# A windowed-attention and gated feed-forward kernel: first loads on two hardware queues, the second half masked by products

## The chip, the cores and the metric

One of the eight cores of a Trainium2 chip runs the whole program. The metric is device time in microseconds (us): the kernel before takes 258.63 us, the median of three runs (257.68 to 258.73).

## The reference

Attention over four batches, eight heads, 768 positions and 64 values per head, then a feed-forward layer. A query sees the last 96 positions up to its own and the first eight positions of all ("global"); a slope per head times the distance is taken from the scores.

```python
scores = scale * np.matmul(q, k.transpose(0, 1, 3, 2))
dist = np.where(is_global & ~is_local, float(n_local), np.abs(rel))
scores = np.where(is_global | is_local, scores - slopes * dist, -1e9)
a = softmax(scores); x = a @ v          # (B, H, S, D), then laid out as 3072 x 512
out = (np.maximum(x @ w_gate, 0) * (x @ w_val)) @ w_out
```

The weights are 512 x 1536 twice and 1536 x 512; the output is 3072 x 512 in float32.

## The kernel before, in words

The 3072 tokens are eight chunks of 384 (two halves `s` of each batch). A chunk goes through scores, exponential, weighted sum of values, normalisation (logarithm, exponential of its negative, product: lines 450 to 455) into `xT`, and then through the feed-forward pieces `gate`, `val` and `outp` (L477, L487, L496). A gate is four matmuls over the four 128-row parts of `xT`, one per pair of heads, so its fourth matmul needs the last pair of the chunk. `gate` is followed by a ReLU on ScalarE (L480), `val` by a product on VectorE (L489).

The order of all instructions is written out by hand; each engine works its own list in order. From chunk 2 on, a function `weave` lays attention pieces between feed-forward pieces. Chunks 0 and 1 are different, since nothing is there yet to lie beside them. All of the change is in these two.

**Chunk 0** (the code from L540 to L595). Its keys and queries come in three pairs of loads on the SyncE queue (`load_first`, L181: heads 0-1, 2-3, 4-7, keys before queries), its values with one load on GpSimd's queue (L216). GpSimd builds an index table `rel`, the distances `dd` (L198 to L202), the identity `ident` (L206), the table `sidx`, and then issues the load of the values. VectorE patches eight rows of `dd`, makes `diag` tiles (identity times a slope, L232) and casts the loaded rows to bfloat16 (L284); TensorE turns them (L275, "transposes"); copies bring them into `kT` and `qT` (L262 to L264, L292). `first_scores` (L311) puts two things into one PSUM tile `s_ps`: `diag` times `dd`, which adds slope times distance and the mask (L321), and then keys times queries (L330). ScalarE takes the exponential into `ef` (L336). `first_values` (L307) picks the value rows with products by `sel`. `first_av` (L440) sums the values (once with ones, for the denominator); `first_norm` follows. `keep_busy` (L538) are matmuls on zeros.

In the written order the transposes of heads 4-5 (`first_keys(2)`) stand ahead of the scores of heads 2-3. GpSimd casts heads 6-7 and issues the first two weight loads (L153) and the loads of chunk 1 (L562).

**Chunk 1** (L605 to L619). The pieces of its attention stand between the first twelve feed-forward pieces of chunk 0 (`F[0]` to `F[11]`: gate and val of six of the twelve column groups). `second_keys` (K) is 12 transposes, two copies on VectorE (L300, L301) and three on GpSimd (L266 to L268). SC is `first_scores` for one of two groups of a head pair. PSUM has two `ff` tiles, one `s_ps` tile and four `t` tiles in this stretch, so that the next scores wait for the exponential of the last. After it, the steady part begins with the gate of group 6 of chunk 0.

Chunks from 2 on use no `diag`: they multiply the exponential by a table `m_all` on VectorE (L393). That table is made by eight exponentials on ScalarE (`make_mask`, L242), woven between the feed-forward pieces that follow chunk 1 (L635).

Of the kernel before, what the change touches and what calls it, by code (L numbers as in the profile page):

```python
# [15 lines left out]
def kernel(  # L16
# [87 lines left out]
    def w_of(t, dc, fc):  # L104
        f = fc % GW
        return t[fc // GW][:, dc, f * 128 : (f + 1) * 128]
# [68 lines left out]
    def rows_of(src, s, h0, h1):  # L175
        b, half = divmod(s, 2)
        return src[b, h0:h1, half * QH : (half + 1) * QH, :].rearrange("h (p n) d -> p h (n d)", n=NN)

    def load_first(h0, h1):
        for i, src in enumerate((k, q)):  # L180
            nc.sync.dma_start(out=kq0[:, i, h0:h1, :], in_=rows_of(src, 0, h0, h1))  # L181

    load_first(0, 2)
    load_first(2, 4)
# [1 line left out]
    nc.scalar.preload_act_table_set("natural_log_exp_and_others")  # L186

    zeros = firstp.tile([128, 512], BF16)
    nc.vector.memset(zeros.bitcast(mybir.dt.uint32), 0)
    nc.vector.memset(ident, 0.0)  # L190
    nc.vector.memset(ones, 1.0)


# [1 line left out]
    rel = firstp.tile([128, NN, WQ], FP32)  # L195
    sub = firstp.tile([128, NN, WQ], FP32)
    near = [firstp.tile([NG, NN, WQ], FP32, name=f"near{i}") for i in range(2)]
    nc.gpsimd.iota(rel, [[1, NN], [NN, WQ]], base=NG, channel_multiplier=-1,  # L198
                   allow_small_or_imprecise_dtypes=True)
    nc.gpsimd.affine_select(out=sub, in_=rel, compare_op=ALU.is_ge, fill=BIG, base=NG,  # L200
# [5 lines left out]
    nc.gpsimd.affine_select(out=ident, in_=ident, compare_op=ALU.not_equal,  # L206
                            fill=1.0, base=0, pattern=[[-1, 128]],
                            channel_multiplier=1)
# [25 lines left out]
    def clear_keys(p):  # L234
        nc.vector.memset(kT[0][p][:, 3, 32:128].bitcast(mybir.dt.uint32), 0)
        nc.vector.memset(kT[0][p][:, 6, NG + 48 : 128].bitcast(mybir.dt.uint32), 0)

    def make_sel(n):
        nc.vector.tensor_scalar(sel[:, n], sidx, float(n), None, op0=ALU.is_equal)
# [71 lines left out]
    def first_scores(s, p, g):  # L311
        half = s % 2
        spans_ = [by[half, j] for j in steps_of[half][g]]
        ps = psum["s"].tile([128, 2, 512], FP32, name="s_ps")
        es = ef_pool.tile([128, 2, 360], BF16, name=f"ef{g}")
        cols = sum(NN * w for _, _, w, _ in spans_)
        qd = qTb[s][:, p, 0, :].rearrange("d (n t) -> d n t", n=NN)
        for e in range(2):
            c = 0
            for i, (j, a, w, m) in enumerate(spans_):  # L320
                nc.tensor.matmul(ps[:, e, c : c + NN * w].rearrange("k (n t) -> k n t", n=NN),  # L321
                                 lhsT=diag[:, 2 * p + e],
                                 rhs=dd[:, 0 if j == 0 else 1, :, m : m + w],
                                 start=(i == 0), stop=False, skip_group_check=True)
                c += NN * w
        c = 0
        for i, (j, a, w, m) in enumerate(spans_):
            for e in range(2):
                r = slice(64 * e, 64 * e + 64)
                nc.tensor.matmul(ps[:, e, c : c + NN * w].rearrange("k (n t) -> k n t", n=NN),  # L330
                                 lhsT=kT[0][p][r, j, :], rhs=qd[r, :, a : a + w],
                                 start=False, stop=(i == len(spans_) - 1),
                                 skip_group_check=True)
            es_of[s, p, j] = (es, c)
            c += NN * w
        nc.scalar.activation(es[:, :, 0:cols], ps[:, :, 0:cols], AF.Exp, bias=0.0, scale=scale)  # L336

    def piece_cast_k(s, p):
        nc.gpsimd.tensor_copy(  # L339
# [126 lines left out]

    out_v = out.rearrange("(s p n) d -> s n p d", p=128, n=NN)

    def ffn_pieces(c):
        ht = ht_pool.tile([128, N_FC, QH], BF16, name="ht")  # L470
        st = {}

        def gate(fc):
            xT = xT_of[c]
            psg = psum["ff"].tile([128, 512], FP32, name="ff_ps")
            for dc in range(N_DC):
                nc.tensor.matmul(psg[:, 0:QH], lhsT=w_of(wg, dc, fc), rhs=xT[:, dc, :],  # L477
                                 start=(dc == 0), stop=(dc == N_DC - 1))
            gr = gr_pool.tile([128, QH], BF16, name="grelu")
            nc.scalar.activation(gr, psg[:, 0:QH], AF.Relu, bias=0.0, scale=1.0)  # L480
            st["gr"] = gr

        def val(fc):
            xT = xT_of[c]
            psv = psum["ff"].tile([128, 512], FP32, name="ff_ps")
            for dc in range(N_DC):
                nc.tensor.matmul(psv[:, 0:QH], lhsT=w_of(wv, dc, fc), rhs=xT[:, dc, :],  # L487
                                 start=(dc == 0), stop=(dc == N_DC - 1))
            nc.vector.tensor_tensor(ht[:, fc, :], psv[:, 0:QH], st["gr"], op=ALU.mult)  # L489

        def outp(n, part):
            if part == 0:
                st["o"] = psum["ff"].tile([128, 512], FP32, name="ff_ps")
            ps2 = st["o"]
            for fc in range(part * N_FC // 2, (part + 1) * N_FC // 2):
                nc.tensor.matmul(ps2, lhsT=ht[:, fc, n * 128 : (n + 1) * 128],  # L496
                                 rhs=wo_sb[:, fc, :],
                                 start=(fc == 0), stop=(fc == N_FC - 1))
            if part == 1:
                osb = osb_pool.tile([128, DM], FP32, name="osb")  # L500
# [52 lines left out]
    clear_keys(1)  # L553
    keep_busy(3)
    first_keys(1, A)
    keep_busy(2)
    first_cast(3, 0, P)
    load_w_group(0)
    first_cast(3, 1, P)
    for h0 in (0, 4):  # L560
        for i, src in enumerate((k, q)):
            nc.gpsimd.dma_start(out=kq1[:, i, h0 : h0 + 4, :], in_=rows_of(src, 1, h0, h0 + 4))  # L562
    for j in (4, 5, 6, 3):
        load_v(0, j)
    first_scores(0, 0, 0)
    make_sel(1)
    first_cast(2, 0, V)
    first_cast(2, 1, V)
    clear_keys(2)
    first_scores(0, 0, 1)  # L570
    first_keys(2, V)
    make_sel(2)
# [32 lines left out]
    stack = open_psum(ff=2, s=1, t=4)  # L605
    f1_0, f2_0 = ffn_pieces(0)
    f1_1, f2_1 = ffn_pieces(1)
    F = [f for _, f in f1_0]
    K = [lambda p=p: second_keys(p) for p in range(HP)]

    def SC(p, g):
        return lambda: first_scores(1, p, g)
# [77 lines left out]
```

## Time and profile before

| What | Time |
|---|---|
| median of three runs | 258.63 us |
| the profiled execution | 259.5 us, its span 257.7 us |
| TensorE busy | 245.1 us (95% of the span) |
| ScalarE, VectorE, GpSimd busy | 155.0, 130.0, 91.9 us |
| the gate of the last pair's `xT` for chunk 0 (L477 at its fourth matmul) | starts at 24.06 us |
| the gate of group 6, where the steady part begins | starts at 45.08 us |
| last matmul's copy (L501) | starts at 253.94 us |

All times in the views are microseconds from the start of the span. Busy times are sums over an engine's instructions. A row of the timeline gives start, length, engine, line, operation, output and input, and in brackets the idle time before it with what ended it. A row of a table by windows gives for each engine the busy time and the number of instructions in that stretch; PEclk is the granted TensorE clock, 1.00 being full. A row of the chain of waits gives start and length of a piece of the chain that ended last.

### The profile page before, as it was taken

The numbers are of one execution on the slowest core, as the hardware profiler recorded it, in microseconds if no ns is written. First come the engines' busy times: TensorE is split into PE (matmuls) and PEld (weight loads), VectorE is DVE, ScalarE is ACT, GpSimd is POOL, SyncE is SP. The second block draws the span as 40 slices with busy tenths as digits, with TensorE's granted clock in tenths as the row PEclk, the third lists the DMA queues.
The fourth block names the chain that finished last, engine by engine and source line by source line (L and its number), as shares of the span: only waits on it lengthen the run. The fifth ranks groups of instructions, "written<-read, shape, count | busy, mean of one in ns | idle before, by whom it ended". The sixth has DMA issues, their size and how long they took to land.

```text
span 257.7 us, 4900 instructions
## 1 busy us (share of the span) xinstructions
PE 245.1 (95%) x1757; PEld 143.3 (56%) x1766; DVE 130.0 (50%) x330; ACT 155.0 (60%) x308; POOL 91.9 (36%) x227
## 2 busy tenths in 40 slices
PE   7797988999999999999999999999999999999993
PEld 3355654665554566655665566556665566556641
DVE  6764405374643377625674376624763457614410
ACT  2536466833577577756875577747774677643311
POOL 6674494066844606800744236500640000000000
PEclk9889999999999999999999999999999999999999
DMA  6999999958966993775693987926491200021012
GB/s 177 158 197 178 206 138 150 256 143 152 268 109 172 185 299 78 135 81 179 175 112 53 201 248 123 107 84 211 116 145 41 81 3 0 1 84 41 0 43 81
DMA packets 80232, 33.59 MB, mean 130 GB/s; under 512 B 58192, under 2 KB 77136, under 8 KB 80208
## 3 DMA queue, kind: packets, MB, share of 16 engines
q1 hardware_dynamic: 48464, 24.57, 37.7%
q0 software_dynamic: 31744, 8.71, 32.9%
q8 instruction: 14, 0.23, 0.4%
q14 instruction: 10, 0.08, 0.1%
HBM read 28.41 MB, written 6.29 MB: 135 GB/s over the span
## 4 chain that ended last, share of the span: by engine, by line
PE 83%; ACT 6%; DVE 5%; DMA 3%; issue 1%; SPq 1%; ACTq 0%; DVEq 0%
PE ff_ps L496 24%; PE ff_ps L487 22%; PE ff_ps L477 22%; PE av_ps L409 5%; PE qk_ps L381 4%; DMA kq<-in_q_dram 3%; DVE xT L426 2%; PE s_ps L321 2%; ACT ef L336 2%; DVE ht L489 2%; PE t_ps L307 1%; PE s_ps L330 1%; PE t_ps L275 1%; ACT lnd L418 1%; SPq L181 1%
## 5 line engine op out<-in xcount | busy, mean ns | idle before, releaser
L477 PE MATMUL ff_ps<-xT,wg 128*128 128x384 bf16 x384 | 78.4, 326 | 1.6 <-DVE xT L455 0.9
L487 PE MATMUL ff_ps<-xT,wv 128*128 128x384 bf16 x384 | 78.1, 326 | 1.0 <-DVE ht L489 0.8
L480 ACT ACTIVATE grelu<-ff_ps 128x384 bf16<-128x384 f32 x96 | 46.9, 489 | 36.0 <-DVE ht L489 18.6
L489 DVE TENSOR_TENSOR ht<-ff_ps,grelu 128x384 bf16<-128x384 f32 x96 | 53.2, 555 | 28.2 <-PE ff_ps L487 22.8
L496 PE MATMUL ff_ps<-wo_sb,ht 128*128 128x512 bf16 x279 | 66.3, 379 | 0.5
L426 DVE TENSOR_TENSOR xT<-av_ps,rcp 64x384 bf16<-64x384 f32 x48 | 26.6, 555 | 46.1 <-ACT rcp L423 41.6
L477 PEld LDWEIGHTS <-wg 128*128 128x128 bf16 x384 | 36.1, 97 | 24.7 <-issue 1.7
L487 PEld LDWEIGHTS <-wv 128*128 128x128 bf16 x384 | 36.1, 97 | 24.7 <-issue 3.2
L393 DVE TENSOR_TENSOR es<-es,m_all 128x432 bf16<-128x432 bf16 (+5 forms) x108 | 33.5, 339 | 22.9 <-ACT es L384 22.4
L384 ACT ACTIVATE es<-qk_ps 128x432 bf16<-128x432 f32 (+2 forms) x72 | 37.8, 528 | 10.7 <-PE qk_ps L381 8.9
L496 PEld LDWEIGHTS <-ht 128*128 128x128 bf16 x288 | 26.9, 97 | 27.8
L339 POOL CAST kc<-ks 128x384 bf16<-128x384 f32 x24 | 12.0, 541 | 59.1 <-DMA ks<-in_k_dram 47.2
L418 ACT ACTIVATE lnd<-av_ps 64x384 f32<-64x384 f32 x48 | 23.3, 485 | 11.0 <-PE av_ps L409 10.4
L501 ACT COPY osb<-ff_ps 128x512 f32<-128x512 f32 x24 | 14.0, 585 | 24.4 <-PE ff_ps L496 23.5
L381 PE MATMUL qk_ps<-qT,kT 128*128 128x432 bf16 (+5 forms) x108 | 24.7, 286 | 0.0
L409 PEld LDWEIGHTS <-vbuf 128*128 128x128 bf16 x216 | 18.1, 98 | 8.2 <-issue 0.7
L136 POOL DMA_DIRECT2D vbuf<-in_v_dram x25 | 21.6, 875 | 1.7 <-DMA wv<-in_moe_w_val_dram 1.1
L409 PE MATMUL av_ps<-es,vbuf 128*128 128x216 bf16 (+4 forms) x216 | 21.1, 226 | 0.5 <-DVE xT L426 0.5
L336 ACT ACTIVATE ef<-s_ps 128x720 bf16<-128x720 f32 (+2 forms) x16 | 11.2, 708 | 11.6 <-PE s_ps L330 11.4
L347 POOL CAST qz<-qs 128x192 bf16<-128x192 f32 x48 | 14.8, 357 | 4.3 <-DMA qs<-in_q_dram 4.3
L381 PEld LDWEIGHTS <-kT 128*128 128x128 bf16 x108 | 10.6, 98 | 7.8
L423 ACT ACTIVATE rcp<-lnd 128x384 f32<-128x384 f32 x24 | 12.5, 523 | 0.8
(80 smaller groups left out, 142.7 us busy)
## 6 DMA issues: line engine op xcount, KB each, us to landing
out_dram<-osb SPq DMA_DIRECT2D x24, 256.0 KB
ks<-in_k_dram SPq DMA_DIRECT2D x6, 768.0 KB
qs<-in_q_dram SPq DMA_DIRECT2D x6, 768.0 KB
vbuf<-in_v_dram POOLq DMA_DIRECT2D x21, 120.0 KB, 4.7
wg<-in_moe_w_gate_dram POOLq DMA_DIRECT2D x3, 512.0 KB, 8.0
wv<-in_moe_w_val_dram POOLq DMA_DIRECT2D x3, 512.0 KB, 10.2
wo_sb<-in_moe_w_out_dram POOLq DMA_DIRECT2D x1, 1536.0 KB, 15.1
kq<-in_k_dram SPq DMA_DIRECT2D x2, 192.0 KB
```

The costliest lines, as they stand in the source:

```text
L136: nc.gpsimd.dma_start(out=v_dst(b, NG + r0, NG + r0 + n, j), in_=v[b, :, KT * j + r0 : KT * j + r0 + n, :].rearrange("h p d -> p h d"))
L381: nc.tensor.matmul(ps[:, c : c + n_], lhsT=kt[:, j, :], rhs=qd[:, :, :, a : a + w], start=True, stop=True)
L384: nc.scalar.activation(es[:, 0:cols], ps[:, 0:cols], AF.Exp, bias=0.0, scale=scale)
L393: nc.vector.tensor_mul(e4, e4, mk)
L409: nc.tensor.matmul(av3[:, :, a : a + w], lhsT=vb[:, j, z0 : z0 + 128], rhs=es[:, c : c + NN * w].rearrange("k (n p) -> k n p", n=NN), star ...
L418: nc.scalar.activation(ln[o0 : o0 + 64], av[d0 : d0 + 64, 0:QH], AF.Ln, bias=0.0, scale=1.0)
L426: nc.vector.tensor_tensor(xT_of[s][r, p, :], av_of[s, p, e_][r, 0:QH], rc[r], op=ALU.mult)
L477: nc.tensor.matmul(psg[:, 0:QH], lhsT=w_of(wg, dc, fc), rhs=xT[:, dc, :], start=(dc == 0), stop=(dc == N_DC - 1))
L480: nc.scalar.activation(gr, psg[:, 0:QH], AF.Relu, bias=0.0, scale=1.0)
L487: nc.tensor.matmul(psv[:, 0:QH], lhsT=w_of(wv, dc, fc), rhs=xT[:, dc, :], start=(dc == 0), stop=(dc == N_DC - 1))
L489: nc.vector.tensor_tensor(ht[:, fc, :], psv[:, 0:QH], st["gr"], op=ALU.mult)
L496: nc.tensor.matmul(ps2, lhsT=ht[:, fc, n * 128 : (n + 1) * 128], rhs=wo_sb[:, fc, :], start=(fc == 0), stop=(fc == N_FC - 1))
```

## The change

There are four edits, and nothing changes from the gate of group 6 on except that the eight `make_mask` exponentials are gone from there.

- **First loads.** Keys go on SyncE's queue and queries on ScalarE's. The load of the values moves to the head of GpSimd's list, and `ident` to the place after it. The clears of `kT` move from VectorE to GpSimd. The first weight loads (`load_w_group(0)`) and half of chunk 1's loads move ahead of GpSimd's casts. The cast of heads 2-3's queries moves from ScalarE to VectorE.
- **Order in chunk 0.** The scores of heads 2-3 now stand ahead of the transposes of heads 4-5. Two of the eight `make_mask` move to ScalarE's start.
- **Masks by products.** For chunk 1, `first_scores` leaves out its `diag` matmuls; `first_masks` multiplies the exponentials by `m_all` on VectorE. The other six `make_mask` stand between the pieces of chunk 1.
- **Split first gate, and an order of chunk 1.** The first three matmuls of `gate(0)` and `val(0)` run as `begin`, the fourth of each after it. The first sums of chunk 1 (`AV[0]`) stand between the last scores.

The program's lists agree: TensorE has 40 matmuls and their weight loads less, VectorE 20 products more. ScalarE has three load issues more and one cast less, SyncE three loads less.

```diff
     def load_first(h0, h1):
-        for i, src in enumerate((k, q)):
-            nc.sync.dma_start(out=kq0[:, i, h0:h1, :], in_=rows_of(src, 0, h0, h1))
+        for i, (src, eng) in enumerate(((k, nc.sync), (q, nc.scalar))):
+            eng.dma_start(out=kq0[:, i, h0:h1, :], in_=rows_of(src, 0, h0, h1))
...
+    nc.gpsimd.dma_start(out=v3, in_=rows_of(v, 0, 0, H))
+    nc.gpsimd.affine_select(out=ident, in_=ident, ...)
     nc.gpsimd.iota(rel, [[1, NN], [NN, WQ]], base=NG, ...)
...
-    nc.gpsimd.affine_select(out=ident, in_=ident, ...)
...
-    nc.gpsimd.memset(vbuf[0][:, NT - 1, :].bitcast(mybir.dt.uint32), 0)
-    nc.gpsimd.dma_start(out=v3, in_=rows_of(v, 0, 0, H))
+    for p in range(HP):
+        nc.gpsimd.memset(kT[0][p][:, 3, 32:128].bitcast(mybir.dt.uint32), 0)
+        nc.gpsimd.memset(kT[0][p][:, 6, NG + 48 : 128].bitcast(mybir.dt.uint32), 0)
...
-        for e in range(2):
+        for e in range(2) if half == 0 else ():
             c = 0
             for i, (j, a, w, m) in enumerate(spans_):
                 nc.tensor.matmul(ps[...], lhsT=diag[:, 2 * p + e], ...)
...
+    def first_masks(s, p, g):
+        for j in steps_of[s % 2][g]:
+            _, a, w, m = by[s % 2, j]
+            es, c = es_of[s, p, j]
+            for_all = es[:, :, c : c + NN * w]
+            mk = m_all[:, 2 * p : 2 * p + 2, 0 if j == 0 else 1, :, m : m + w]
...
+            nc.vector.tensor_mul(for_all, for_all, mk)
...
+        def begin():
+            product(wg, "g", 0, 0, N_DC - 1)
+            product(wv, "v", 0, 0, N_DC - 1)
+        begin_of[c] = (begin, lambda: gate(0, N_DC - 1), lambda: val(0, N_DC - 1))
...
     keep_busy(9)
+    load_w_group(0)
     make_diag(0)
     make_diag(1)
-    clear_keys(0)
+    make_mask(0)
+    make_mask(1)
     first_cast(0, 0, V)
     first_cast(0, 1, V)
     make_sel(0)
     first_cast(1, 0, V)
-    first_cast(1, 1, A)
+    first_cast(1, 1, V)
     first_keys(0, A)
...
     first_keys(1, A)
     keep_busy(2)
-    first_cast(3, 0, P)
-    load_w_group(0)
-    first_cast(3, 1, P)
+    first_scores(0, 0, 0)
+    make_sel(1)
+    first_scores(0, 0, 1)
+    make_sel(2)
+    first_cast(2, 0, V)
+    first_cast(2, 1, V)
     for h0 in (0, 4):
         for i, src in enumerate((k, q)):
             nc.gpsimd.dma_start(out=kq1[:, i, h0 : h0 + 4, :], ...)
+        if h0 == 0:
+            first_cast(3, 0, P)
+            first_cast(3, 1, P)
...
     first_scores(0, 1, 0)
     for h in range(4, H):
         make_diag(h)
-    clear_keys(3)
     first_scores(0, 1, 1)
+    first_keys(2, V)
     first_values(0, V)
     first_keys(3, V)
...
-    F = [f for _, f in f1_0]
+    F = list(begin_of[0]) + [f for _, f in f1_0[2:]]
+    M = [lambda h=h: make_mask(h) for h in range(H)]
...
-    for f in (F[0], F[1], K[0], F[2], K[1], SC(0, 0), F[3], SC(0, 1), K[2], F[4], SC(1, 0), K[3], F[5],
-              SC(1, 1), SC(2, 0), F[6], SC(2, 1), AV[0], SC(3, 0), N[0], AV[1], SC(3, 1), N[1], F[7],
-              lambda: load_qk_after(2), AV[2], F[8], N[2], AV[3], F[9], N[3], F[10], F[11]):
+    for f in (F[0], F[1], F[2], M[2], M[3], K[0], F[3], K[1], SC(0, 0), F[4], SC(0, 1), M[4], K[2], SC(1, 0), F[5],
+              M[5], SC(1, 1), K[3], F[6], M[6], SC(2, 0), AV[0], N[0], M[7], SC(2, 1), F[7], AV[1], N[1],
+              SC(3, 0), F[8], SC(3, 1), AV[2], N[2], lambda: load_qk_after(2), F[9], AV[3], N[3],
+              F[10], F[11], F[12]):
         f()
...
-    weave(f1_1[G[0]], spread([(0.0, lambda h=h: make_mask(h)) for h in range(H)], 0.0, 1.0))
+    weave(f1_1[G[0]])
```

In the new list SC(p, g) is the scores followed by `first_masks`, F[0] is `begin`, F[1] and F[2] are the fourth matmuls of the first gate and val with their ReLU and product.

More of the change, by code (lines that the diff above doesn't have):

```diff
@@ L188 @@
     zeros = firstp.tile([128, 512], BF16)
+    nc.vector.memset(ident, 0.0)
     nc.vector.memset(zeros.bitcast(mybir.dt.uint32), 0)
-    nc.vector.memset(ident, 0.0)
     nc.vector.memset(ones, 1.0)
@@ L197 @@
     near = [firstp.tile([NG, NN, WQ], FP32, name=f"near{i}") for i in range(2)]
+    nc.gpsimd.dma_start(out=v3, in_=rows_of(v, 0, 0, H))
+    nc.gpsimd.affine_select(out=ident, in_=ident, compare_op=ALU.not_equal,
+                            fill=1.0, base=0, pattern=[[-1, 128]],
+                            channel_multiplier=1)
     nc.gpsimd.iota(rel, [[1, NN], [NN, WQ]], base=NG, channel_multiplier=-1,
@@ L205 @@
                             channel_multiplier=1)
-    nc.gpsimd.affine_select(out=ident, in_=ident, compare_op=ALU.not_equal,
-                            fill=1.0, base=0, pattern=[[-1, 128]],
-                            channel_multiplier=1)
     sidx = firstp.tile([128, 4, 128], FP32, name="sidx")
@@ L232, in make_diag @@
         nc.vector.tensor_scalar(diag[:, h], ident, -slopes[h] / scale, None, op0=ALU.mult)
-    def clear_keys(p):
-        nc.vector.memset(kT[0][p][:, 3, 32:128].bitcast(mybir.dt.uint32), 0)
-        nc.vector.memset(kT[0][p][:, 6, NG + 48 : 128].bitcast(mybir.dt.uint32), 0)
     def make_sel(n):
@@ L331, in first_scores @@
                                  lhsT=kT[0][p][r, j, :], rhs=qd[r, :, a : a + w],
-                                 start=False, stop=(i == len(spans_) - 1),
+                                 start=(i == 0 and half == 1), stop=(i == len(spans_) - 1),
                                  skip_group_check=True)
@@ L336, in first_scores @@
         nc.scalar.activation(es[:, :, 0:cols], ps[:, :, 0:cols], AF.Exp, bias=0.0, scale=scale)
+    def first_masks(s, p, g):
[4 more added lines that the diff above has]
+            mk = m_all[:, 2 * p : 2 * p + 2, 0 if j == 0 else 1, :, m : m + w]
+            if w == WQ:
+                mk = mk.rearrange("k e n p -> k e (n p)")
+            else:
+                for_all = for_all.rearrange("k e (n p) -> k e n p", n=NN)
+            nc.vector.tensor_mul(for_all, for_all, mk)
     def piece_cast_k(s, p):
@@ L467 @@
     out_v = out.rearrange("(s p n) d -> s n p d", p=128, n=NN)
+    begin_of = {}
     def ffn_pieces(c):
@@ L471, in ffn_pieces, with product, gate @@
         st = {}
[L473 to L477, printed above, removed]
+        def product(w, key, fc, d0, d1):
+            if d0 == 0:
+                st[key] = psum["ff"].tile([128, 512], FP32, name="ff_ps")
+            for dc in range(d0, d1):
+                nc.tensor.matmul(st[key][:, 0:QH], lhsT=w_of(w, dc, fc), rhs=xT_of[c][:, dc, :],
                                  start=(dc == 0), stop=(dc == N_DC - 1))
+        def gate(fc, d0=0):
+            product(wg, "g", fc, d0, N_DC)
+            psg = st["g"]
             gr = gr_pool.tile([128, QH], BF16, name="grelu")
@@ L481, in gate, with val @@
             st["gr"] = gr
[L483 to L488, printed above, removed]
+        def val(fc, d0=0):
+            product(wv, "v", fc, d0, N_DC)
+            psv = st["v"]
             nc.vector.tensor_tensor(ht[:, fc, :], psv[:, 0:QH], st["gr"], op=ALU.mult)
@@ L552 @@
     make_diag(3)
-    clear_keys(1)
     keep_busy(3)
@@ L562 @@
             nc.gpsimd.dma_start(out=kq1[:, i, h0 : h0 + 4, :], in_=rows_of(src, 1, h0, h0 + 4))
+        if h0 == 0:
+            first_cast(3, 0, P)
+            first_cast(3, 1, P)
+    nc.gpsimd.memset(vbuf[0][:, NT - 1, :].bitcast(mybir.dt.uint32), 0)
     for j in (4, 5, 6, 3):
         load_v(0, j)
[L565 to L572, printed above, removed]
     first_scores(0, 1, 0)
@@ L607, with run @@
     f1_1, f2_1 = ffn_pieces(1)
-    F = [f for _, f in f1_0]
+    F = list(begin_of[0]) + [f for _, f in f1_0[2:]]
     K = [lambda p=p: second_keys(p) for p in range(HP)]
+    M = [lambda h=h: make_mask(h) for h in range(H)]
     def SC(p, g):
-        return lambda: first_scores(1, p, g)
+        def run():
+            first_scores(1, p, g)
+            first_masks(1, p, g)
+        return run
     AV = [lambda p=p: first_av(1, p) for p in range(HP)]
     N = [lambda p=p: first_norm(1, p) for p in range(HP)]
-    for f in (F[0], F[1], K[0], F[2], K[1], SC(0, 0), F[3], SC(0, 1), K[2], F[4], SC(1, 0), K[3], F[5],
-              SC(1, 1), SC(2, 0), F[6], SC(2, 1), AV[0], SC(3, 0), N[0], AV[1], SC(3, 1), N[1], F[7],
-              lambda: load_qk_after(2), AV[2], F[8], N[2], AV[3], F[9], N[3], F[10], F[11]):
+    for f in (F[0], F[1], F[2], M[2], M[3], K[0], F[3], K[1], SC(0, 0), F[4], SC(0, 1), M[4], K[2], SC(1, 0), F[5],
+              M[5], SC(1, 1), K[3], F[6], M[6], SC(2, 0), AV[0], N[0], M[7], SC(2, 1), F[7], AV[1], N[1],
+              SC(3, 0), F[8], SC(3, 1), AV[2], N[2], lambda: load_qk_after(2), F[9], AV[3], N[3],
+              F[10], F[11], F[12]):
         f()
```

## Prediction

> **What bounds the kernel now.** I read the page first: TensorE is busy 95% of the span, and the chain of waits is 83% TensorE. Then the chain in order of time. From 45.08 us on it is gates, vals and outputs end to end, 0.65 us for four matmuls, down to the last copy. No edit touches that, so the change is worth what it takes off the 45.08 us ahead of it. There the chain reads:
>
> ```profile
> 3.31 6.69 DMA kq<-in_q_dram
> 10.02 0.55 DVE qk L284
> ...
> 18.45 0.77 ACT ef L336
> ...
> 33.33 0.46 PE s_ps L321 x6
> 33.78 0.27 PE s_ps L330 x6
> 34.06 0.02 issue
> 34.08 0.74 ACT ef L336
> 34.82 0.04 issue
> 34.86 0.47 PE s_ps L321 x4
> ```
>
> Chunk 0 waits for the last queries (issued at 3.31, used at 10.02). Its middle is TensorE's, and from 18.45 it is ScalarE's: exponentials, logarithms and reciprocals up to the last `xT` at 24.01. Chunk 1 is a loop through one PSUM tile: `diag` matmuls, scores, exponential, `diag` again, each waiting for the last.
>
> Third, the table by windows, in steps of 3.41 us, because the granted clock changes at these steps:
>
> ```profile
> 4.61:8.02 3.41, 2.93 (x27) 1.54 (x25) 1.90 (x10) 1.37 (x3) 0.28 (x1) 1.00 0.99 268
> 8.02:11.44 3.42, 1.80 (x26) 1.07 (x22) 2.38 (x11) 1.23 (x2) 2.45 (x4) 1.00 0.97 122
> 11.44:14.85 3.41, 3.41 (x25) 1.93 (x21) 2.86 (x13) 1.34 (x2) 3.41 (x6) 0.50 1.04 163
> 21.68:25.09 3.41, 2.23 (x20) 1.11 (x21) 1.58 (x3) 2.17 (x5) 1.53 (x3) 1.00 2.13 165
> 25.09:28.50 3.41, 3.34 (x48) 2.13 (x46) 1.99 (x6) 1.22 (x2) 1.60 (x6) 1.00 1.25 207
> ```
>
> The second number is TensorE's busy time, the third from the end its granted clock. A window with 1.80 us of work (53%) is followed by one at half clock; one with 2.23 us (65%) is not. Last I read the rows of single shapes, for the products that chunk 1 gets:
>
> ```profile
> L393 DVE TENSOR_TENSOR es<-es,m_all 128x432 bf16<-128x432 bf16 x36 | 14.8, 413 | 11.2 <-ACT es L384 10.8
> L393 DVE TENSOR_TENSOR es<-es,m_all 128x144 bf16<-128x144 bf16 x12 | 2.8, 232 | 5.3 <-ACT es L384 5.3
> L242 ACT ACTIVATE m_all<-dd 128x432 bf16<-128x432 bf16 x8 | 4.0, 554 | 0.0
> ```
>
> The last number ahead of the second bar is the mean of one in ns.
>
> **Chunk 0, part by part.** *GpSimd's start.* The load of the values costs its row, 1.06 us, and `ident` 0.25 (2.31 to 2.56, start to start); both now stand ahead of `dd`, which ends at 3.67 instead of 2.36. VectorE patches `dd` and makes two `diag` before its first cast, 1.03 us from 2.39 to 3.42, less 0.10 for the clears that leave. So the first cast starts at 4.6, 1.2 later. Most of this is covered: before, the copy of the first keys stood until 6.98 for ScalarE, which was casting queries at 6.06. That cast is now VectorE's, 0.4 us. Two casts and a `sel` (0.94, 0.65) bring VectorE to 6.2, the casts of heads 2-3 to 7.1, and the copies of the first keys (0.53, 0.17, 0.18, overlapping: 0.7) to 7.8. First scores at 8.1 instead of 7.79: 0.3 lost, not yet on the path. ScalarE's two `make_mask` (1.0) lie at 4.7 to 5.7, ahead of its first copy. GpSimd's eight clears (0.07 start to start) end near 5.0; then it issues the first weights, at 5.0 and 5.8 instead of 9.62 and 10.39.
>
> *Landing of the loads.* Before, keys and queries of heads 4-7 were waited for until 8.99 and 10.02, and the values landed 8.1 us after their issue at 3.84, at 11.9. Now values, keys and queries start together: three issues of 0.47 on each of two queues end at 2.2 instead of 3.8, but the bytes are the same 1.97 MB, and at the 235 GB/s of the stretch from 5 to 10 us they take 8.4 us. Shared evenly, all three end together. Bounds: 9.0 (the earliest landing before) and 14.7, if the weights' 1.05 MB come in between as well (3.0 MB at 235 GB/s, 12.8 us from 1.9). I take 11.0, nearest to the 10.02 and 11.9 of the two landings that now share.
>
> The Trainium skill, page "DMA: Bandwidth & Descriptors", section "Issuing engines are not separate DMA queues", speaks against this edit: the queues feed the same 16 engines, and a second one saves only time of issue. By it the last queries would land at 10.0 at best, which would add 1.0 us to the gain.
>
> *After the landing.* TensorE's list is shorter there, because the scores of heads 2-3 (0.6 and 0.55) have gone ahead, into the wait. From 11.0: casts 0.85, transposes 0.4, value product 0.65 (ends 12.8), transposes of heads 6-7 0.34, scores of heads 4-5 0.6 (they wait for VectorE's copies until 13.4; end 13.7), values 0.65, scores 0.5, two values 1.3, scores of heads 6-7 0.6: 16.7. Before, these ended at 18.41. So ScalarE's tail begins at 16.8 instead of 18.45 and is the same from there: **1.6 us** less, the last `xT` at 22.4. This holds at full clock. By my count TensorE has 2.3 us of work in 8.02 to 11.44 (four score groups, about 0.6 each), 67%: nearer to the 65% that kept the clock than to the 53% that lost it. At half clock this tail takes 1.4 us longer.
>
> **Chunk 1.** *Removed:* the eight L321 pieces of the chain between 26.7 and 38.5: 0.40, 0.47, 0.30, 0.31, 0.46, 0.47, 0.46, 0.47, together 3.3 us. *Split gate:* after the last `xT` stood 0.32 + 0.65 us of gate and val; now two matmuls of 0.16. The other six run while TensorE stands idle for `xT` (2.23 of 3.41 us busy in that window): 0.65 less. *Added on ScalarE:* six `make_mask`, 0.45 start to start (two in 1.00 us). Two lie beside the transposes of the first second-half keys; four stand between exponentials, where ScalarE then sets the pace: 1.8 on the path. *Added on VectorE:* per pair five products, 0.41 + 0.23 + 0.24 and 0.37 + 0.34 us by L393's shapes, 6.4 us in all. VectorE is busy 7.7 of 20 us from 25 to 45, so they fit; but the copies of keys and queries and the products `xT` and `ht` queue behind them, and the last two ahead of the sums are uncovered: 0.6. Sum: 3.3 + 0.65 - 1.8 - 0.6 = **1.55 us** less.
>
> Bounds: 3.95 with everything added hidden; -1.2 if the other two masks (0.9) and three more groups of products (0.6 each) come on the path. I take 1.55, since ScalarE's share is counted in full.
>
> The Trainium skill, page "SBUF — State Buffer", section "Who interferes with whom", says that a VectorE instruction with two inputs in SBUF and a GpSimd instruction that reads SBUF exclude each other. That would set the 20 products against the 12 key copies of GpSimd (0.93 us a pair); at worst 3.7 us of waiting, which would use up the gain in chunk 1. L393's rows are measured beside GpSimd work already, but no row shows the wait alone.
>
> *After 45 us.* The masks gone from there free ScalarE, which does not bound. Queries of chunk 2 are turned by DMAs whose issue ends at 63.06, and first used at 66.52; 3 us less makes that tight, if their loads (issued at 41.76) do not move up too. They are issued after the second normalisation of chunk 1 as before, so they should: nothing, at worst 1 us.
>
> **Sum.** 1.6 + 1.55 = 3.15 us off the profiled execution's 259.5: 256.35. That execution is 0.87 over the median of the runs, 258.63, on which I put the forecast: **255.5**.
>
> **Rivals.**
> - *The clock falls again* (16%). For it: 67% is close to 65%, and my count may be high. It gives 1.6 - 1.4 + 1.55 = 1.75 off: 256.9. About two thirds of this case is over 0.5% (1.3 us) faster.
> - *Loads faster than before* (13%): two queues fill the engines better, landing at 9.5 or earlier; the tail is then bound by VectorE's copies. 1.5 more: 254.0.
> - *The two queues do not do what they say; mild collision* (12%): landing at 11.5 to 12.5 and a lost clock. 3.15 - 1.4 - 0.5 to 1.5: 1.25 to 0.25 off, around 257.9.
> - *Slower* (10%): values and first weights are served ahead of the last keys and queries, which land at 14.7. For it: GpSimd's loads are issued 3 and 4.6 us earlier than now. Against: the weights are issued at 5.0, well after the last of the six loads at 2.2, so most of these are ahead of them. From 11.0 to 14.7 is 3.7 us later, and TensorE idle costs the clock, 1.4: 3.15 - 3.7 - 1.4 = -2.0, so 260.6. It decides against the change once the landing passes 12.8 with the clock lost, or 14.1 with it kept.
> - The forecast itself has 49%.
>
> Half a per cent, 1.3 us, is about what a measurement of this kernel can tell from no change. Faster by more: 0.49 + 0.13 + 0.11 + 0.01 = 0.74; within: 0.05 + 0.11 = 0.16; slower: 0.10. The range runs from 253.8 (the faster loads) to 258.4 (the mild collision); it leaves out the slower case and the tails beyond, some 2 in 10.
>
> **What would show it.** The last `xT` of chunk 0 near 22.4 instead of 24.01; the fourth matmul of the first gate right behind it; exponentials of chunk 1 about 1.4 us apart; the gate of group 6 near 42.0; granted clock 1.00 from 11 to 15 us. Wrong if the last keys' cast starts past 12.8, if VectorE's products are the releaser of most waits from 23 to 42, or if TensorE waits near 63 us.

## The result, and the profile after

The changed kernel takes 256.26 us, the median of four runs (255.94 to 256.75). The kernel before, run beside it, takes 258.34 (257.68 to 258.73). The ratio is 0.9924, its 95% interval 0.9895 to 0.9952: faster by 0.5 to 1.0%. The forecast of 255.5 was 0.8 us too low, and 256.26 lies within its range. The profiled execution takes 256.75 us, its span is 255.0 (before: 259.5 and 257.7). Ratios leave out runs that lie over 1.5% above the fastest of their kernel; where that matters, with one hardware queue below, the times themselves are read.

The total came out nearly as forecast, but not from the terms forecast. The chain of waits of the changed kernel (start, length, piece), in order of time:

```profile
3.58 0.61 POOL dd L206
...
8.60 0.28 PE s_ps L328 x4
...
10.78 0.21 PE s_ps L328 x4
10.99 0.44 PE t_ps L273 x6
...
16.26 0.77 ACT ef L334
...
21.26 0.57 DVE xT L465
...
28.31 0.45 ACT m_all L240
28.76 0.66 ACT ef L334
29.42 0.45 ACT m_all L240
29.87 0.70 ACT ef L334
...
37.17 0.64 PE ff_ps L489 x4
37.81 16.73 DMA qs<-in_q_dram
54.56 1.50 SPq L360
...
60.15 3.33 DMA qT<-qz
```

Read it from the top. GpSimd's `dd` and the first scores (8.60) stand on the chain, and no wait for a load does before 37.81. The first score group of chunk 0's last pair gets its exponential at 16.26 (before: 18.45), and the last `xT` ends at 21.82 (24.01). No L319 piece (`diag`) stands in chunk 1; in its place stand exponentials with `m_all` between them. Then comes what the chain before did not have: a load of 16.73 us, the queue that turns the loaded rows (L360, L364), and the arrival of `qT`. From 37.81 to 63.48 the end is set by DMAs, not by TensorE.

The timeline shows where TensorE pays, with the idle time before the row in brackets, and GpSimd's first cast of chunk 2's keys; below it SyncE's queue in the same kernel, and the same rows of the kernel before:

```profile
51.07 1.86 POOL L349 CAST kc<-ks 128x384 bf16<-128x384 f32 x4 [10.69 <-DVE ht L502]
...
63.62 0.34 PE L391 MATMUL qk_ps<-qT,kT 128*128 128x432 bf16 x1 [2.27 <-DMA qT<-qz]
```

```profile
37.34 0.38 SPq L117 DMA_DIRECT2D ks<-in_k_dram  x1
37.81 0.53 SPq L117 DMA_DIRECT2D qs<-in_q_dram  x1
...
52.96 4.41 SPq L360 DMA_TRANSPOSE kN<-kc  x3
57.48 4.01 SPq L364 DMA_TRANSPOSE qT<-qz  x3
```

```profile
41.76 0.38 SPq L117 DMA_DIRECT2D ks<-in_k_dram  x1
...
53.15 1.85 POOL L339 CAST kc<-ks 128x384 bf16<-128x384 f32 x4 [11.80 <-DVE vbuf L141]
...
59.05 4.01 SPq L354 DMA_TRANSPOSE qT<-qz  x3
...
66.52 0.35 PE L381 MATMUL qk_ps<-qT,kT 128*128 128x432 bf16 x1
```

Chunk 2's keys and queries are issued 4.4 us earlier than before (41.76 there). Yet the first cast of these keys starts at 51.07 (before: 53.15), and that of the queries at 54.66 (55.41). From the issue of the keys to their first cast it took 13.7 us instead of 11.4. The brackets of the two casts name VectorE, whose signal came last; that the load decides is shown by run 1, where the same cast follows its load at once.

The windows where the clock had fallen (TensorE's busy time is second, its granted clock third from the end):

```profile
8.02:11.44 3.42, 3.10 (x41) 1.98 (x39) 3.13 (x12) 2.53 (x5) 3.02 (x5) 1.00 1.32 217
11.44:14.85 3.41, 3.41 (x32) 1.85 (x31) 3.16 (x12) 1.62 (x3) 3.41 (x5) 1.00 1.27 203
```

TensorE is busy 3.10 us of the first (1.80 before), and the next is at 1.00 instead of 0.50.

The two executions differ as follows, in positions on their own timelines:

| Stretch | before | after | change |
|---|---|---|---|
| start to the last `xT` of chunk 0 | 24.01 | 21.82 | -2.19 |
| from there to the gate of group 6 | 21.07 | 17.91 | -3.16 |
| from there to the first matmul on chunk 2's queries | 21.44 | 23.88 | +2.44 |
| from there to the end of the span | 191.18 | 191.38 | +0.20 |

The sum is -2.71, the difference of the spans. The steady part began 5.3 us earlier, and nearly half of that was lost at one wait. Theory: the wait is a new bound, set by the loads of chunk 2, which run beside the load of the output weights (issued at 36.07), and it hides what the change won in chunk 1. Rivals: the products and the other edits of chunk 1 are worth little anyway; or the turning of rows by DMA is slow whenever it starts.

### The profile page after: what moved, and what is told of

It reads as the page before. It is cut to its first block, busy times and chain, and to the rows that moved or that the text cites. A ratio compares the mean times of both kernels' runs of the same rounds, so it can differ in the third digit from the quotient of the medians.

```text
span 255.0 us, 4850 instructions
## 1 busy us (share of the span) xinstructions
PE 242.1 (95%) x1726; PEld 140.6 (55%) x1726; DVE 132.4 (52%) x343; ACT 154.8 (61%) x307; POOL 93.7 (37%) x235
## 4 chain that ended last, share of the span: by engine, by line
PE 73%; DMA 8%; ACT 8%; DVE 5%; SPq 2%; issue 2%; POOL 1%; POOLq 0%; ACTq 0%
PE ff_ps L489 35%; PE ff_ps L509 24%; DMA qs<-in_q_dram 7%; PE av_ps L419 5%; PE qk_ps L391 4%; DVE xT L436 2%; ACT ef L334 2%; DVE ht L502 1%; DMA qT<-qz 1%; PE s_ps L328 1%; ACT grelu L496 1%; PE t_ps L305 1%; SPq L360 1%; SPq L364 1%; ACT lnd L428 1%
## 5 line engine op out<-in xcount | busy, mean ns | idle before, releaser
L509 PE MATMUL ff_ps<-wo_sb,ht 128*128 128x512 bf16 x288 | 67.1, 379 | 0.0
L394 ACT ACTIVATE es<-qk_ps 128x432 bf16<-128x432 f32 (+2 forms) x72 | 37.8, 529 | 13.0 <-PE qk_ps L391 11.4
L403 DVE TENSOR_TENSOR es<-es,m_all 128x432 bf16<-128x432 bf16 (+5 forms) x108 | 31.7, 323 | 25.7 <-ACT es L394 25.2
L428 ACT ACTIVATE lnd<-av_ps 64x384 f32<-64x384 f32 x48 | 23.3, 485 | 11.0 <-PE av_ps L419 10.4
## 6 DMA issues: line engine op xcount, KB each, us to landing
out_dram<-osb SPq DMA_DIRECT2D x24, 256.0 KB
```

The lines of the kernel that those rows point to most:

```text
L394: nc.scalar.activation(es[:, 0:cols], ps[:, 0:cols], AF.Exp, bias=0.0, scale=scale)
L403: nc.vector.tensor_mul(e4, e4, mk)
L428: nc.scalar.activation(ln[o0 : o0 + 64], av[d0 : d0 + 64, 0:QH], AF.Ln, bias=0.0, scale=1.0)
```

## The experiments

Each kernel was compared with runs of the kernel before on the same chip (medians 259.38 for runs 1 to 4, 258.83 for 5 to 8, 258.50 for 9 to 11, 258.49 for 12; each of these four groups ran on a chip of its own). "Last xT to last xT" is from chunk 0's last `xT` to chunk 1's: 19.95 us before, 16.76 after.

**1. Output weights out of the way.** The changed kernel, with the output weights' load moved from ahead of `weave` to after the query casts:

```diff
-    load_w(wo_sb, moe_w_out, 0, DM)
...
+    early_2 = early_pieces(2)
+    early_2.insert(11, (0.0, lambda: load_w(wo_sb, moe_w_out, 0, DM)))
...
```

> The changed kernel with one move: GpSimd issues the load of the output weights (1536 KB) after its casts of chunk 2's queries instead of ahead of them. My theory: the 2.27 us that TensorE waits for chunk 2's turned queries in the changed kernel come from the loads of chunk 2's keys and queries sharing the DMA engines with these weights from 41 to 52 us. Then the first cast of chunk 2's keys starts before 47 us instead of at 51.07, the wait is 0 to 0.3, the span is 252.5 to 253.0 instead of 255.0, and the time is 253.9 to 254.6. Rival: the turning DMAs themselves, or their place in SyncE's list, set the wait; then it stays at 1.5 or more and the time within 0.7 of 256.26. Second rival: the output weights are now late themselves, and TensorE waits for them at its first output matmul, near 62 us.

Measured: 262.59 us, ratio 1.0107 (1.0071 to 1.0143): slower, where 253.9 to 254.6 was expected. Its chain of waits:

```profile
37.33 5.47 DMA ks<-in_k_dram
...
50.13 7.23 SPq L364
57.40 10.87 DMA qT<-qz
68.41 0.52 PE qk_ps L391
```

Without the output weights beside them the keys of chunk 2 land 5.47 us after their issue, and are cast from 42.92, 8.2 us earlier. That part of the theory holds. But now the weights, issued at 48.10 and landing 15.3 us later, run beside the turning of the queries: one issue takes 7.23 us (1.24 for the one before it), the last piece 10.87 (3.33 above). The next loads of keys and queries, issued from 61.91 on, share the last part of this. TensorE waits 7.1 us, and its clock is at about half from 65.7 to 72.5. So this run shows what held the keys back, but is no cure.

**2. The masks back as diag matmuls.** The changed kernel with chunk 1's `diag` matmuls back, no products, and the masks made after chunk 1 as before:

```diff
-        for e in range(2) if half == 0 else ():
+        for e in range(2):
...
-            first_masks(1, p, g)
```

> The changed kernel with the masks of chunk 1 undone: the diag matmuls are back, the products gone, all eight make_mask exponentials back behind chunk 1. My theory: the steady part starts about 2.5 us later than the changed kernel's 39.74 (the 3.16 us that chunk 1 gained less 0.65 for the split gate), near 42.2; but TensorE's wait for chunk 2's queries falls from 2.27 to 0.3 or less, because these land when the DMAs let them. So the time grows by 0.2 to 0.8 only, 256.5 to 257.0. Rival: what the products bring carries through to the end; then the time grows by about 2.5, to 258.8.

Measured: 256.73 us, ratio 0.9909 (0.9875 to 0.9942), not to be told from the changed kernel. The ReLU of group 6 is 1.6 us later (42.20 against 40.59), the first matmul on chunk 2's queries not (63.35 against 63.62), and the wait for them is 0.4 us instead of 2.27. The products bring the gate of group 6 forward by 1.6 us, and the wait takes that.

**3. One queue for the first loads.** The changed kernel with the queries issued by SyncE again:

```diff
-        for i, (src, eng) in enumerate(((k, nc.sync), (q, nc.scalar))):
+        for i, (src, eng) in enumerate(((k, nc.sync), (q, nc.sync))):
```

> The changed kernel with the queries' first loads back on SyncE's queue, the values still first on GpSimd's. If a second queue saves issue time only, the last keys and queries are cast within 0.3 us of the changed kernel's 9.69 and 10.3 us, and the last xT of chunk 0 ends at 21.8 to 22.2. If two queues fill the DMA engines better, the last queries land 0.5 to 1.5 us later and the last xT ends at 22.3 to 23.3. In both cases the time hardly moves, 256.0 to 256.8, as long as TensorE waits for chunk 2's queries.

Measured: 257.18 us in the profiled run, 263.25, 263.31 and 263.69 in the three others. In the profiled run the last cast starts at 11.28 (10.52 with two queues) and the last `xT` ends at 22.77 (21.82). The expected 256.0 to 256.8 was missed by all four, by three of them far; runs 10 and 12 take this up.

**4. The clock alone.** The kernel before with eight matmuls on zeros ahead of the transposes of heads 4-5:

```diff
+    keep_busy(8)
     first_keys(2, V)
```

> The kernel before with eight more matmuls on zeros between the first two score groups of chunk 0 and the transposes of heads 4-5, where TensorE waits for the loads. My theory: the 3.41 us at half clock from 11.44 cost the kernel before 1.0 to 1.5 us; with the clock kept, the last xT of chunk 0 ends at 22.5 to 23.0 instead of 24.01, and the time is 1.0 to 1.5 less than that of the kernel before. Rival: the landing and the order set chunk 0's end; then the last xT stays within 0.3 of 24.01.

Measured: 258.40 us, ratio 0.9964 (0.9941 to 0.9986). The clock stays at 1.00, and the last `xT` ends at 23.27: 0.74 earlier, less than expected.

The clocks on record say more. Each run has a mean granted clock. Of the 71 runs of the kernel before in the four groups, 39 have 0.997 to 1.000 and 32 have 0.991 to 0.993; group by group the medians are 258.1 to 258.4 for the first kind and 259.4 to 259.6 for the second. So an execution in which the clock falls takes 1.1 to 1.5 us longer, and the profiled one of the kernel before (259.5, clock 0.992) is one of these. Run 4 keeps its clock in all ten runs and takes what the kernel before takes whenever it keeps it (258.35 in this group). Between a third of chunk 0's 2.19 us (0.74, this profile) and two thirds (1.5, the times) is thus clock. A late landing in the same executions isn't told apart from it.

**5. Early loads.** If the wait hides the gain, loads issued in time must bring it out. The changed kernel, with chunk 2's loads moved within chunk 1's list. They are issued at 24.95 us now; from 26 to 38 us the DMA engines carry 216 to 282 GB/s with them, 111 to 207 in the changed kernel:

```diff
-    for f in (F[0], F[1], F[2], M[2], M[3], K[0], F[3], K[1], SC(0, 0), F[4], SC(0, 1), M[4], K[2], SC(1, 0), F[5],
+    for f in (F[0], F[1], F[2], M[2], M[3], K[0], F[3], K[1], lambda: load_qk_after(2), SC(0, 0), F[4], SC(0, 1), M[4], K[2], SC(1, 0), F[5],
...
-              SC(3, 0), F[8], SC(3, 1), AV[2], N[2], lambda: load_qk_after(2), F[9], AV[3], N[3],
+              SC(3, 0), F[8], SC(3, 1), AV[2], N[2], F[9], AV[3], N[3],
```

> The changed kernel with the loads of chunk 2's keys and queries issued 10 us earlier (near 27 us, ahead of the scores of chunk 1, instead of 37.3). Theory (2.27 us of the change's gain is lost to the wait for the turned queries, because their loads share the DMA engines with the output weights): the first cast of chunk 2's keys starts near 43 instead of 51.07, the turning DMAs end well before TensorE wants them, no wait of TensorE between 55 and 66 us, the ReLU of group 6 stays near 40.6, first matmul on chunk 2's queries near 61.3, time 2.3 below the changed kernel: near 254.0. Rival 1 (turning is what is slow, beside the output weights, whenever it starts): TensorE waits 2 us or more for the same queries, time as the changed kernel's or above, 256 to 258. Rival 2 (the early loads hold back the weights of groups 1 and 2, which are loaded from 20 to 34 us): TensorE waits at a gate or val between 33 and 45 us, and the gain is given back there.

Measured: 254.39 us (253.85 to 255.59), ratio 0.9856 (0.9828 to 0.9884). SyncE's queue and the first matmul on chunk 2's queries:

```profile
24.95 0.38 SPq L117 DMA_DIRECT2D ks<-in_k_dram  x1
25.42 0.52 SPq L117 DMA_DIRECT2D qs<-in_q_dram  x1
...
42.32 4.53 SPq L360 DMA_TRANSPOSE kN<-kc  x3
46.96 6.18 SPq L364 DMA_TRANSPOSE qT<-qz  x3
```

```profile
61.34 0.35 PE L391 MATMUL qk_ps<-qT,kT 128*128 128x432 bf16 x1
```

The turning ends at 53.1 instead of 61.5, that matmul has no wait in front of it, and it runs 2.28 us earlier: the whole of the 2.27. The ReLU of group 6 stays (40.73), so no weights were held back. Theory confirmed: at that matmul in full size, in the median by 1.9 us (256.26 to 254.39). The first rival is half right: beside the output weights (issued at 36.22, landing 14.2 us later) the turning is slower here too, 6.18 us for the issues of the queries against 4.01, but it starts early enough. The ratio lies below that of the changed kernel, interval and all.

**6. Early loads, masks back as diag matmuls** (the edits of runs 2 and 5 together).

> As the run with the early loads, but with chunk 1's masks put back as diag matmuls into its scores (no products, the masks made later, as before the change). With the wait at the end of the stretch the products' 1.6 us (ReLU of group 6 at 42.20 against 40.59) did not show in the time. Theory (the wait hid it): now it shows, 1.6 us slower than the run with the early loads, near 255.6, and TensorE does not wait for chunk 2's queries. Rival (the products are worth nothing by the end, whatever the wait): same time as the run with the early loads within 0.5 us.

Measured: 256.09 us (255.21 to 256.99), ratio 0.9914 (0.9892 to 0.9937): 1.7 us slower than run 5, where run 2 had shown nothing. TensorE does not wait for `qT`. Last `xT` to last `xT` is 18.25 us against 16.75. So the products, with the mask exponentials that they need, are worth 1.5 to 1.7 us once the end can feel it.

**7. Early loads, first gate not split.**

```diff
-    F = list(begin_of[0]) + [f for _, f in f1_0[2:]]
+    F = [lambda: None] + [f for _, f in f1_0]
```

> As the run with the early loads, but the first gate and val start only after the last xT of chunk 0 (the split undone). The prediction gave the split 0.65 us. Theory: ReLU of group 6 and the end 0.65 later than with the early loads, near 254.6. Rival (chunk 1 is set by ScalarE, so TensorE's six early matmuls fill a gap that would be there later anyway): 0 to 0.2 later.

Measured: 254.34 us, ratio 0.9851 (0.9826 to 0.9877): as run 5. Last `xT` to last `xT` is 16.95 us, 0.2 more. The rival is right: here the split is worth 0.2 us, not 0.65.

**8. The kernel before with early loads** (the control: the edit of run 5 in the list of the kernel before).

> The kernel before the change with the same loads of chunk 2 issued near 28 us instead of 41.8. It had no wait for the turned queries. Theory: no gain, within 0.5 us of the kernel before, since the loads were not late there. Rival (early loads help by themselves, through the use of the DMA engines): 1.5 to 2.5 us faster, which would mean that the gain of the first run is not the change's own wait.

Measured: 258.91 us, ratio 1.0015 (0.9988 to 1.0043): nothing. The early loads cure a wait that the change made.

**9. The order of chunk 1 alone.** Run 8 with chunk 1's pieces lined up as in the changed kernel, without its other edits:

```diff
-    for f in (F[0], F[1], K[0], F[2], K[1], lambda: load_qk_after(2), SC(0, 0), F[3], SC(0, 1), K[2], F[4], SC(1, 0), K[3], F[5],
-              SC(1, 1), SC(2, 0), F[6], SC(2, 1), AV[0], SC(3, 0), N[0], AV[1], SC(3, 1), N[1], F[7],
-              AV[2], F[8], N[2], AV[3], F[9], N[3], F[10], F[11]):
+    for f in (F[0], F[1], K[0], F[2], K[1], lambda: load_qk_after(2), SC(0, 0), F[3], SC(0, 1), K[2], SC(1, 0), F[4],
+              SC(1, 1), K[3], F[5], SC(2, 0), AV[0], N[0], SC(2, 1), F[6], AV[1], N[1],
+              SC(3, 0), F[7], SC(3, 1), AV[2], N[2], F[8], AV[3], N[3],
+              F[9], F[10], F[11]):
```

> The kernel before with the early loads, and with the order of chunk 1's pieces as the change has it (sums of a pair between the score groups of the next, gates moved), but with diag matmuls, no products, masks made later and no split gate. From chunk 0's last xT to chunk 1's last xT the kernel before takes 19.95 us, the changed one 16.76; without products and split it still takes 18.24 (the run with the diag matmuls back). Theory (the prediction's sum for chunk 1 missed the order: it priced the pieces that go and come, not how they are lined up): this run takes 18.2 to 18.6 us, 1.4 to 1.7 less than before, and the time falls by as much, to about 257.2. Rival (the diag matmuls and their waits are all of it, and the order is worth nothing by itself): 19.7 to 20.0 us, time as the kernel before.

Measured: 257.54 us, ratio 0.9954 (0.9929 to 0.9978). Last `xT` to last `xT` is 18.71 us against 19.96 in run 8: 1.25 less, somewhat under the 1.4 expected. ScalarE's timeline shows how, first in run 8 and then here, from the last exponential of the scores on:

```profile
37.06 0.75 ACT L336 ACTIVATE ef<-s_ps 128x720 bf16<-128x720 f32 x1
37.71 0.48 ACT L450 ACTIVATE lnd<-t_ps 128x384 f32<-128x384 f32 x1
...
39.67 0.48 ACT L450 ACTIVATE lnd<-t_ps 128x384 f32<-128x384 f32 x1
...
40.62 0.47 ACT L450 ACTIVATE lnd<-t_ps 128x384 f32<-128x384 f32 x1
```

```profile
37.70 0.77 ACT L336 ACTIVATE ef<-s_ps 128x720 bf16<-128x720 f32 x1 [0.82 <-PE s_ps L330]
38.37 0.48 ACT L450 ACTIVATE lnd<-t_ps 128x384 f32<-128x384 f32 x1
...
39.69 0.48 ACT L450 ACTIVATE lnd<-t_ps 128x384 f32<-128x384 f32 x1
```

Three pairs are still to be normalised after the last exponential in the old order, two in the new. The tail from there to the last `xT` falls from 5.18 us to 3.61.

**10. Early loads, one queue** (the edits of runs 3 and 5).

> The run with the early loads (254.39), with the first queries put back on SyncE's queue: one hardware queue for the six first loads. Theory (two queues bring the last queries in 0.76 us earlier, as the earlier run with one queue showed: last cast 11.28 against 10.52, last xT 22.77 against 21.82): last xT 0.7 to 1.0 later, time 255.2 to 255.5. Rival 1 (a second queue saves only the time of issue, 1.4 us of three issues of 0.47, which the transfer hides): last xT within 0.3 us, time within 0.4. Rival 2 (one queue has a slow mode of its own, as three timed runs near 263.5 beside a profiled run at 257.18 suggest): most timed runs again 5 us or more above.

Measured: 259.17 us, its twelve runs between 255.29 and 261.09, nearest to the second rival. The lower six alone, 255.29 to 259.11, give a ratio of 0.9959 (0.9914 to 1.0003), so they too are above run 5's (0.9828 to 0.9884). The profiled one (260.16) is among the upper six; it has GpSimd's casts of heads 6-7 here, keys and then queries:

```profile
11.51 0.66 POOL L282 CAST qk<-kq 128x384 bf16<-128x384 f32 x1 [2.63 <-DMA kq<-in_k_dram]
15.21 0.70 POOL L282 CAST qk<-kq 128x384 bf16<-128x384 f32 x1 [3.04 <-DMA kq<-in_q_dram]
```

In this execution the last queries come 4.5 us later than in run 5 (10.69), the clock falls to 0.50 from 8.1 to 18.3 us, and the last `xT` ends at 27.54 instead of 21.97.

**11. Early loads, values later** (two queues; the values' load behind GpSimd's tables and clears, at 3.97 instead of 1.25 us).

> The run with the early loads, with the values' load issued by GpSimd at its old place, after the select chains and the clears, about 2 us later. Theory (the values were given the engines early at no cost to keys and queries, and the first value product waits for them): last keys' cast 0 to 0.5 earlier, GpSimd's dd ready 1.1 earlier, values landing near 12.5 instead of 11.2, last xT 0 to 0.7 later than 21.97, time 254.4 to 255.1. Rival (the values take the engines from the last keys and queries): the last cast starts 1 us or more earlier, the last xT 0.5 us or more earlier, time near 253.6.

Measured: 254.28 us (253.75 to 257.56), ratio 0.9839 (0.9804 to 0.9873): as run 5. GpSimd's cast of the last queries starts at 9.21 instead of 10.69, VectorE's last cast at 10.04, and the last `xT` ends 0.44 earlier. So by these two profiles the early values hold the queries back by some 1.5 us, as the rival has it, but the time does not show it. No gain of the values' early load is seen.

**12. Early loads, one queue, values later** (the fourth corner).

> The fourth corner of two edits, on the kernel with the early loads: one hardware queue for the first six loads and the values issued at their old, later place. So far: two queues, values first 254.39; two queues, values later 254.28; one queue, values first 259.17 (last cast at 15.21 in its profile). Theory (the values' load, when it is ahead and only one hardware queue stands against it, takes the place of the last keys and queries; the second queue guards against that and does little else): with the values later one queue is nearly as good, last cast at 10.5 to 11.3, last xT 22 to 23, time 254.4 to 255.6. Rival (one queue is slow by itself, whatever GpSimd loads beside it): last cast past 13, time 257 to 260.

Measured: 255.25 us (254.03 to 256.66), ratio 0.9868 (0.9828 to 0.9909); last cast at 11.17 (GpSimd's, of the last queries, at 9.55), last `xT` at 22.39. All lie in the ranges of the theory: one queue is slow only with the values ahead.

| | values first | values later |
|---|---|---|
| two queues | 254.39 | 254.28 |
| one queue | 259.17 | 255.25 |

That the values take the place of the queries is not shown, however: in the profile of run 10 the values land late themselves, at 11.6 us (10.4 in run 5), and the first weights at 15.4, with the last queries. Why the bad executions with one queue are bad stays open.

## Why the prediction was right in time and wrong in its sum

- **The forecast's side and size.** 3.15 us were forecast off the profiled execution; 2.75 came off (259.5 to 256.75). The agreement is partly luck: 5.3 us were won and 2.4 lost again. The step from 256.35 to the median forecast of 255.5 was wrong: the 0.87 us by which the profiled execution lies above its median are the price of its fallen clock (run 4), which the gain in chunk 0 already counts. Without that step the sum stands at 256.35, beside a measured median of 256.26, though with terms in it that cancel.
- **Chunk 0** (1.6 us forecast, 2.19 in the profiles). Most steps held: last loads at about 10.5 (11.0 taken), the clock at 1.00 (TensorE busy 3.10 us in its window, where 2.3 were counted), the last pair's exponential at 16.26 (16.8). But "First scores at 8.1 ... not yet on the path" did not: they came at 8.53, and the chain runs through them and through `dd` at 3.58, not through a load. It is close, since the last cast of queries ends at 10.87 and TensorE turns them at 10.93. The profile of before had an unlucky start, too: in run 8, with the same code there, the last `xT` ended at 22.28 with no fall of the clock. The usual gain in chunk 0 is therefore smaller. Run 5's 4.44 us on the medians less chunk 1's 3.2 leaves about 1.2; against the runs of the kernel before that keep the clock (258.27 in that group) it is 0.7.
- **Chunk 1** (1.55 forecast, 3.16 measured): the mis-sized term. Masks as products instead of `diag` matmuls were priced at 3.3 - 1.8 - 0.6 = 0.9 and are worth 1.5 (run 6). The split gate was priced at 0.65 and is worth 0.2 (run 7). The order was given no term and is worth 1.25 (run 9), the largest miss. The runs line up, last `xT` to last `xT`: 19.96 (run 8), 18.71 with the order (run 9), 18.25 with the split and chunk 0's edits (run 6), 16.75 with the products (run 5). The steps of 1.25, 0.46 and 1.50 are the whole 3.2; so the split is worth up to 0.46 without the products and 0.2 with them. The products' time was right: the five means of L346 (396, 358, 326, 253, 205 ns) make 6.2 us for four pairs, 6.4 forecast.
- **"After 45 us … nothing, at worst 1 us"**: the step that failed. It assumed that loads issued earlier land earlier. They were issued 4.4 us earlier, into the output weights' load, which is issued only 1.0 us earlier than before (36.07 against 37.03), and the keys were cast only 2.1 us earlier. The prediction also took the end of the last turning issue (63.06) for the landing, which gives 3.5 us to spare until 66.52. After the change the last of these issues starts at 60.15 and its rows arrive 3.33 later; with the same 3.33 from 61.72, the start before, they landed at 65.05 there (an estimate), with 1.5 to spare. The issue moved up by 1.6 us, TensorE by 5.2 at this point; less the 1.5 and the 1.6, about the wait is left. Cost: 2.27 us, shown by runs 5 and 8; run 1 shows what held the keys. A wait of TensorE near 63 us was one of the prediction's own signs of being wrong, and it came.
- **The rivals.** Neither the clock nor a collision came. The slower rival's landing (14.7) is what one queue gives in the profile of run 10 (last cast 15.21); no profile with two queues shows it. What decides between the near and the far times of one queue is open: in run 3 the profiled run was a near one. The prediction's reading of windows (53% busy, then half clock; 65%, then full) is no rule, either: in run 3 the window from 4.61 to 8.02 is 49% busy (1.66 us) and the clock stays at 1.00, in run 10 it is as busy (1.68) and the next is at 0.51.
- **The Trainium skill's rules.** "DMA: Bandwidth & Descriptors", section "Issuing engines are not separate DMA queues", has a second queue save only time of issue. With the values later that fits well enough (255.25 against 254.28, in the size of the 1.4 us of three issues of 0.47). With the values first it does not: 4.8 us on the medians, where the measurement decides. For "SBUF — State Buffer", section "Who interferes with whom", the worst case of 3.7 us did not come: GpSimd's twelve key copies beside chunk 1 went from 417, 273 and 228 ns to 417, 312 and 287, 0.4 us in all.

## What to carry to other kernels

When a change brings a stretch forward, list what the next stretch waits for, and work out the landing of each load from what shares the DMA engines with it at its new time, not from its issue. Before putting a forecast on the profiled execution, see whether its clock is that of most runs. A gain that the time doesn't show may be hidden rather than absent: remove the wait, then measure each part again. Price the order of a hand-written list as a term of its own, by what is still to do after the last step of the slow engine.

## What the runs showed of the hardware

- DMAs that turn rows are slowed by a 1.5 MB load beside them. The three issues of chunk 2's queries take 4.01 us in the changed kernel (57.48, the weights landed at 52.8), 6.18 in run 5 (46.96, the weights landing at 50.4) and 13.02 in run 1 (48.84, the weights issued at 48.10).
- A load issued 4.4 us earlier was cast only 2.1 us earlier beside that load: 13.7 us from issue to first cast, against 5.47 from issue to landing without it (run 1).
- On the same code the clock may fall or not: 32 of the 71 runs of the kernel before have a mean clock of 0.991 to 0.993 (medians 259.4 to 259.6 us), 39 of 0.997 to 1.000 (258.1 to 258.4).
- For the same six loads, of the same bytes, GpSimd casts the last queries at 10.69 on two hardware queues (run 5); on one at 10.64 in one profile (run 3) and 15.21 in another (run 10), with GpSimd's 384 KB load issued at 1.25 us. With that load at 3.97 it is 9.21 and 9.55. How the engines choose between queues was not tried further.
